# A planner's computed order replaced by a written table, with 24 GpSimd maxima tied to VectorE's place

## The chip, the cores and the metric

The kernel runs on one core of one Trainium2 chip. The time is that of one execution on the device, in microseconds (us); three executions of the kernel before gave 1046.39, 1047.41 and 1048.51, median 1047.41.

## The reference, cut to what is computed

```python
# attention: batch 8, heads 8, seq 576, head_dim 64, 128 features
def phi(x):
    proj = einsum('bhsd,df->bhsf', x, w_phi)
    proj = proj - max(abs(proj), axis=-1)
    return concatenate([exp(proj), exp(-proj)], axis=-1)
q_p, k_p = phi(q), phi(k)
kv  = einsum('bhsf,bhsd->bhfd', k_p, v);  z = sum(k_p, axis=2)
attn = einsum('bhsf,bhfd->bhsd', q_p, kv) / (einsum('bhsf,bhf->bhs', q_p, z) + 1e-6)
# feed-forward on 4608 tokens, 512 -> 2048 -> 512, weights as 64-bit words
x = attn as (batch*seq, heads*head_dim)
return gelu(x @ w_in) @ w_out
```

## The kernel before

The program is a list of 3,662 operations, created in a fixed order and numbered from 0: 914 of TensorE (one may be up to 80 matmuls), 933 of ScalarE, 1,209 of VectorE, 68 of GpSimd and 538 of SyncE, which issues nearly all DMAs. `Plan.op` notes for each its engine, cost, buffers and rank. `Plan.order` then simulates all engines with the costs written at the top of the class, and picks at each step the operation of lowest rank that can go; the ranks contain a hand-written table DELAY of offsets. `Plan.emit` sorts by the planned start and writes the instructions; every engine keeps that order. Semaphore waits between engines follow from the data and buffers alone. So what a run does is set by five orders, one for each engine, and by how long each operation waits for another engine.

The work has these parts, named as in the traces:

- **Attention, k side** (`k_unit`, `k_quad`): TensorE projects a part of k (pk, in PSUM); VectorE takes the maximum over features (mx, L465) and subtracts it (ek, L401), both reading PSUM; ScalarE takes two exponentials (L470); TensorE sums k with v (kv), ScalarE copies it to kvn.
- **Attention, q side** (`q_front`, `q_pair`, `q_rest`): TensorE projects q transposed (pq), ScalarE copies it to SBUF (pc, L395), GpSimd takes the maximum over partitions (mb, L539, `partition_all_reduce`), VectorE subtracts (pc<-pc,mb, two operands in SBUF), ScalarE takes two exponentials (ef, L544), TensorE forms numerators (pn) and, for the first three batches, denominators (dn), which ScalarE copies to xo and do. Later batches sum denominators on GpSimd (db, L550). A maximum has one of three sizes: 288 columns (batch 0), 512 ("main") and 64 times four ("rest").
- **Weights** (`split_weight`): each of 32 pieces w_i*, w_o* is loaded (raw), unpacked from 64-bit words by ScalarE (L416) and four VectorE steps (wt, L417, L419, L421, L423), and split in a high and a low part (ScalarE cast, VectorE subtraction at L401). The last piece of w_in is w_i3_3.
- **Feed-forward** (`tokens`, `up`, `block`, and from the ninth block `seven`): for each of 18 blocks of 256 tokens, 12 matmuls for each of 16 column groups (ph), gelu twice on ScalarE, their difference on VectorE (gl, L401, reading PSUM), and po. Batch after batch of attention feeds it.
- **Weight sums** (`sums_of_weights`): ts, on VectorE and ScalarE, used by the later blocks.

Of the kernel before, what the change touches and what calls it, by code (L numbers as in the profile page):

```python
# [62 lines left out]
class Plan:  # L63


    HOP = {"pe": 0.2, "act": 0.14, "dve": 0.13, "pool": 0.1, "sp": 0.05}
    SAME = {"pe": 0.0, "act": 0.0, "dve": 0.127, "pool": 0.1, "sp": 0.0}
    SWITCH = 1.3

    BEHIND = {"f": 0.1, "k": 0.1, "q": 0.095, "v": 0.09, "w": 0.09, "n": 0.1, "d": 0.05, "z": 0.09}  # L70
    BEFORE = {"f": 0.08, "k": 0.1, "q": 0.1, "v": 0.05, "w": 0.05, "n": 0.05, "d": 0.1, "z": 0.04}
    SHAPE = {"f": 0, "k": 1, "q": 1, "v": 2, "n": 2, "w": 3, "d": 4, "z": 5}
    READS = {"max": 1.15, "add": 2.45, "max main": 2.1, "add main": 4.43, "max rest": 1.05, "add rest": 2.15}
    WRITES = {"max": (1.4, 2.02), "add": (2.75, 3.47), "max main": (2.3, 3.42), "add main": (4.6, 5.97), "max rest": (1.2, 1.83), "add rest": (2.4, 3.1)}
    SPENT = {"max": 2.14, "add": 3.59, "max main": 3.54, "add main": 6.11, "max rest": 1.94, "add rest": 3.23}
    WINDOW = 3.413
    BUSY = 0.8
# [5 lines left out]

    def turn(self, a, b):
        return self.BEHIND[a] + self.BEFORE[b] + (0.09 if a == "f" and b != "d" else 0.0)

# [47 lines left out]
    def order(self, bias):  # L134
        free = dict(self.slots)
        slot_free_at = {t: [0.0] * n for t, n in self.slots.items()}
        turn = dict.fromkeys(self.slots, 0)
        engines = {}
        for o in self.ops:
            engines.setdefault(o.eng, [])  # L140
        clock = dict.fromkeys(engines, 0.0)
        table = [None]
        cand = {e: [] for e in engines}
        for o in self.ops:
            if o.wait == 0:
                cand[o.eng].append(o)
        done = []
        n = len(self.ops)

        gelus, left_at, dma, dge = [0], [0.0], [0.0], [0.9]  # L150
        port = [0.0]

        def start_of(o):
            t = max(clock[o.eng], o.ready)
            if o.table == "exp" and table[0] == "gelu" and gelus[0] % (2 * STICK):
                t = max(t, left_at[0] + PATIENCE)
            seen = {}
            for b in o.bufs:
                if not b.held and b.tag is not None:
                    f, i = slot_free_at[b.tag], seen.get(b.tag, 0)  # L160
                    if len(b.line) <= i or b.line[i] is not b:
                        return None
                    when = f[(turn[b.tag] + i) % len(f)]
                    if when is None:
                        return None
                    t = max(t, when)
                    seen[b.tag] = i + 1
            if o.eng == "dve":
                for a, z, least in port[1:]:
                    if o.port >= least and a <= t < z:  # L170
                        t = z
            return t


        clk = {"i": 0, "full": False, "busy": 0.0}
        last, first = ["f"], {}

        def run(t, work, duty):
            while work > 1e-9:
                i = int(t / self.WINDOW + 1e-9)  # L180
                while clk["i"] < i:
                    use = clk["busy"] / self.WINDOW
                    clk["full"] = use > (0.5 if clk["full"] else self.BUSY)
                    clk["i"] += 1
                    clk["busy"] = 0.0
                speed = 1.0 if clk["full"] else 0.51
                dt = min((i + 1) * self.WINDOW - t, work / speed)
                clk["busy"] += dt * duty
                work -= dt * speed
                t += dt  # L190
            return t

        while len(done) < n:
            best = None
            for e, lst in cand.items():
                if not lst:
                    continue
                opts = []
                for o in lst:
                    t = start_of(o)  # L200
                    if t is not None:
                        opts.append((t, o))
                if not opts:
                    continue
                t0 = min(t for t, _ in opts)
                lim = max(t0, clock[e]) + 0.02
                hold = 0.0
                if e == "pe" and last[0] == "f":
                    t_of = {id(o): max(o.ready, first.setdefault(o.n, t)) for t, o in opts}
                    there = [o for t, o in opts if t <= lim and o.kind != "f"]  # L210
                    if sum(o.cost for o in there) < LUMP and all(lim - t_of[id(o)] < LINGER for o in there):
                        hold = 4000.0
                key = None
                for t, o in opts:
                    if t <= lim:
                        k = o.rank
                        if e == "act" and o.table is not None and o.table != table[0]:
                            k += bias
                        if o.kind != "f":
                            k += hold  # L220
                        if key is None or (k, o.n) < key[0]:
                            key = ((k, o.n), t, o)
                if best is None or key[1] < best[1] or key[1] == best[1] and e == "pool":
                    best = key
            if best is None:
                raise RuntimeError("no operation can go")
            _, t, o = best
            cand[o.eng].remove(o)
            cost = o.cost
            if o.eng == "act" and o.table is not None and o.table != table[0]:  # L230
                cost += self.SWITCH
                table[0] = o.table
            if o.eng == "pe":
                if self.SHAPE[last[0]] != self.SHAPE[o.kind]:
                    cost += self.turn(last[0], o.kind)
                last[0] = o.kind
            o.start = t
            if o.eng == "pool" and o.port:
                t = max(t, port[0])
                a, z = self.WRITES[o.port]  # L240
                port[1:] = [(t, t + self.READS[o.port], 1), (t + a, t + z, 2)]
            o.end = run(t, cost, o.duty) if o.eng == "pe" else t + cost
            if o.nbytes:
                dge[0] = max(dge[0], t) + 0.55
                dma[0] = max(dma[0], dge[0] + 0.75) + o.nbytes / RATE
                o.late = dma[0] + 0.15 + DMASLACK - o.end
            if o.table == "gelu":
                gelus[0] += 1
                left_at[0] = o.end
            clock[o.eng] = o.end  # L250
            if o.eng == "dve" and o.port:
                port[0] = o.end
            for b in o.bufs:
                if b.tag is not None and not b.held:
                    f = slot_free_at[b.tag]
                    b.slot = turn[b.tag]
                    f[b.slot] = None
                    turn[b.tag] = (b.slot + 1) % len(f)
                    b.held = True
                    assert b.line.pop(0) is b  # L260
                b.left -= 1
                if b.left == 0 and b.tag is not None:
                    slot_free_at[b.tag][b.slot] = o.end + o.late + self.HOP[o.eng] + (PESLACK if b.tag in self.banks else 0.0)
            for u in o.users:
                u.wait -= 1
                u.ready = max(u.ready, o.end + o.late + (self.HOP if u.eng != o.eng else self.SAME)[o.eng] + (POOLSLACK if o.eng == "pool" else 0.0) + (PESLACK if u.eng == "pe" and o.eng != "pe" else 0.0))
                if u.wait == 0:
                    cand[u.eng].append(u)
            done.append(o)
        self.done = done  # L270
        return max(o.end + o.late for o in done)

    def emit(self):
        todo = sorted(self.done, key=lambda o: (o.start, o.n))
        parts = [o.part for o in todo if o.eng == "pe"][1:] + [None]
        for o in todo:
            if o.eng == "pe":
                self.then = parts.pop(0)
            if o.reopen and self.turn_over is not None:
                self.turn_over()  # L280
                self.turn_over = None
# [731 lines left out]
SUMSAT = 175.933  # L1013
# [72 lines left out]
```

## Time and profile before

| what | value |
|---|---|
| median of three executions | 1047.41 us |
| the profiled execution | 1048.43 us |
| its span, first to last instruction | 1046.6 us |
| TensorE busy | 1019.6 us |
| VectorE busy | 661.1 us |
| ScalarE busy | 614.5 us |
| GpSimd busy | 276.9 us |
| mean granted TensorE clock | 0.993 |

Times in the trace count from the start of the span; 1.83 us of the profiled execution lie outside it. Lines such as L401 belong to helpers used for many operations, so an operation is known by its tile (ph, mx, wt_o) and its time.

### The profile page before, as it was taken

The numbers are of one execution on the slowest core, as the hardware profiler recorded it, in microseconds if no ns is written. First come the engines' busy times: TensorE is split into PE (matmuls) and PEld (weight loads), VectorE is DVE, ScalarE is ACT, GpSimd is POOL, SyncE is SP. The second block draws the span as 40 slices with busy tenths as digits, with TensorE's granted clock in tenths as the row PEclk, the third lists the DMA queues.
The fourth block names the chain that finished last, engine by engine and source line by source line (L and its number), as shares of the span: only waits on it lengthen the run. The fifth ranks groups of instructions, "written<-read, shape, count | busy, mean of one in ns | idle before, by whom it ended". The sixth has DMA issues, their size and how long they took to land.

```text
span 1046.6 us, 24197 instructions
## 1 busy us (share of the span) xinstructions
PE 1019.6 (97%) x10070; PEld 893.1 (85%) x10070; DVE 661.1 (63%) x1209; ACT 614.5 (59%) x1011; POOL 276.9 (26%) x72
## 2 busy tenths in 40 slices
PE   6889998999999999999999999999999999999998
PEld 5555776878878878897887889999999999999998
DVE  5899999987777854334643433555564556474754
ACT  5788888886768766757755642343243334243433
POOL 2343331373376352326566540000000000000000
PEclk9899999999999999999999999999999999999999
DMA  8775654524534433222321339201111111110000
GB/s 294 216 231 170 208 189 119 164 88 140 162 123 147 152 108 91 67 76 72 97 72 39 97 107 326 60 22 41 44 39 40 43 42 42 41 42 19 24 22 21
DMA packets 87327, 107.11 MB, mean 102 GB/s; under 512 B 29021, under 2 KB 57245, under 8 KB 87217
## 3 DMA queue, kind: packets, MB, share of 16 engines
q1 hardware_dynamic: 86928, 105.30, 32.7%
q8 instruction: 79, 1.29, 0.5%
q14 instruction: 32, 0.25, 0.1%
q10 hardware_dynamic: 288, 0.26, 0.1%
HBM read 75.87 MB, written 29.66 MB: 101 GB/s over the span
## 4 chain that ended last, share of the span: by engine, by line
PE 90%; DVE 5%; ACT 2%; issue 1%; DMA 1%; SPq 0%; DVEq 0%; ACTq 0%
PE ph L360 38%; PE po L360 17%; PE pa L360 10%; PE pb L360 7%; PE kv L360 6%; PE pn L360 4%; PE pk L360 3%; PE pq L360 3%; PE dn L360 1%; DVE wt_i L421 1%; PE pn_rest L360 1%; DMA vt<-in_va_dram 1%; DVE ek L401 0%; DVE wt_i L423 0%; DVE pc L401 0%
## 5 line engine op out<-in xcount | busy, mean ns | idle before, releaser
L360 PE MATMUL ph<-xh,w_i 128*128 128x256 f32 x2304 | 416.6, 278 | 0.0
L360 PEld LDWEIGHTS ph<-xh,w_i 128*128 128x128 f32 x2304 | 357.1, 188 | 9.0 <-issue 5.1
L360 PE MATMUL ph<-xl,w_i 128*128 128x256 f32 x1152 | 319.3, 277 | 0.0
L360 PEld LDWEIGHTS ph<-xl,w_i 128*128 128x128 f32 x1152 | 217.2, 189 | 0.3
L539 POOL PARTITION_ALL_REDUCE mb<-pc x36 | 120.6, 3356 | 202.3 <-ACT pc L395 153.3
L360 PE MATMUL po<-w_o,gh 128*128 128x512 f32 (+1 forms) x519 | 162.4, 395 | 0.0
L550 POOL PARTITION_ALL_REDUCE db<-pc x20 | 124.2, 6212 | 93.7 <-DVE pc L600 89.9
L360 PEld LDWEIGHTS po<-w_o,gh 128*128 128x128 f32 x519 | 93.3, 188 | 30.0 <-issue 8.5
L401 DVE TENSOR_TENSOR sg<-ga 128x256 f32<-128x256 f32 (+1 forms) x240 | 84.3, 376 | 54.1 <-ACT ga L839 50.3
L360 PE MATMUL pa<-w_o,oh 128*128 128x256 f32 x640 | 112.6, 276 | 0.0
L401 DVE TENSOR_TENSOR gl<-ph,gh 128x512 fp32r<-128x512 f32 x64 | 43.5, 687 | 90.7 <-ACT ph L750 90.6
L360 PE MATMUL po<-w_o,gl 128*128 128x512 f32 (+1 forms) x275 | 100.8, 378 | 0.0
L360 PEld LDWEIGHTS pa<-w_o,oh 128*128 128x128 f32 x640 | 96.3, 188 | 0.1
L839 ACT ACTIVATE ga<-ph 128x512 f32<-128x512 f32 x80 | 47.8, 597 | 82.3 <-PE ph L360 52.1
L401 DVE TENSOR_TENSOR ul<-sg,uh 128x384 fp32r<-128x384 f32 x80 | 44.6, 558 | 71.5 <-ACT uh L395 70.3
L360 PE MATMUL pa<-w_o,ol 128*128 128x256 f32 x320 | 88.3, 276 | 0.0
L360 PE MATMUL pb<-tw,uh 128*128 128x256 f32 x464 | 82.9, 276 | 0.1
L544 ACT ACTIVATE ef<-pc 128x1024 f32<-128x1024 f32 (+1 forms) x72 | 68.1, 973 | 14.2 <-DVE pc L401 10.3
L470 ACT ACTIVATE ek<-ek 128x1024 f32<-128x1024 f32 x64 | 67.6, 1059 | 11.1 <-DVE ek L401 10.2
L395 ACT CAST uh<-sg 128x384 fp32r<-128x384 f32 x80 | 41.0, 512 | 50.6 <-PE pb L360 25.3
L360 PEld LDWEIGHTS pb<-tw,uh 128*128 128x128 f32 x464 | 69.9, 188 | 0.3 <-DVE ob L401 0.3
L360 PE MATMUL pn<-ef,kvn 128*64 128x512 f32 (+1 forms) x288 | 64.9, 571 | 1.9 <-ACT do L395 0.8
(93 smaller groups left out, 1591.5 us busy)
## 6 DMA issues: line engine op xcount, KB each, us to landing
vt<-in_va_dram SPq DMA_DIRECT2D x32, 325.0 KB
t_d<-ts SPq DMA_DIRECT2D x40, 256.0 KB
out_dram<-ob SPq DMA_DIRECT2D x34, 256.0 KB
kt<-in_kT_dram SPq DMA_DIRECT2D x32, 256.0 KB
raw_i<-in_w_in_dram SPq DMA_DIRECT2D x16, 512.0 KB
raw_o<-in_w_out_dram SPq DMA_DIRECT2D x16, 512.0 KB
qt<-in_qT_dram SPq DMA_DIRECT2D x28, 256.0 KB
x_d<-xo SPq DMA_DIRECT2D x28, 256.0 KB
```

The lines of the kernel that those rows point to most:

```text
L360: return tc.keep_in_program_order(nc.tensor.matmul(*a, **kw))
L395: op(eng, cost, lambda: nc.scalar.copy(out=dst(), in_=src()), r=r, w=w, **kw)
L401: op(eng, cost, lambda: e.tensor_tensor(out=dst(), in0=a(), in1=b(), op=o), r=r, w=w, **kw)
L421: op("dve", dve(512), lambda: v.scalar_tensor_tensor(out=t(), in0=low(), scalar=29, in1=t(), op0=ALU.logical_shift_right, op1=ALU.bitwise_ ...
L470: op("act", act(256 * n), lambda s=s: nc.scalar.activation(e[s](), e[1](), AF.Exp, scale=1.0 - 2.0 * s), r=[e[1]], w=[e[s]], table="exp", ...
L539: op("pool", plan.SPENT[most], lambda: nc.gpsimd.partition_all_reduce(mb(), pc(), P, bass_isa.ReduceOp.absmax), r=[pc], w=[mb], port=most, ...
L544: op("act", act(2 * n), lambda s=s: nc.scalar.activation(ef[s](), pc(), AF.Exp, scale=1.0 - 2.0 * s), r=[pc], w=[ef[s]], table="exp", **k())
L550: op("pool", plan.SPENT[total], lambda: nc.gpsimd.partition_all_reduce(db(), pc()[:, :2], P, bass_isa.ReduceOp.add), r=[pc], w=[db], port= ...
L839: op("act", act(2 * TB, True) + 0.037, lambda ph=ph, ga=ga: nc.scalar.activation(ga(), ph(), AF.Gelu), r=[ph_all], w=[ga], table="gelu", a ...
```

## The change

`Plan.order` no longer simulates. It reads ORDER, a table of all 3,662 operation numbers, and `Plan.emit` writes them in this order. The ranks, DELAY and the planner's costs are left in part but nothing reads them. The operations themselves, their buffers (HOME is untouched) and their shapes are the same. Place by place, 177 of TensorE's 914 places hold another operation than before, 357 of ScalarE's 933, 442 of VectorE's 1,209, 320 of SyncE's 538, and 2 of GpSimd's 68. The last place that differs on VectorE is the 505th, which runs 422 us after the start in the trace before.

A second table, TOGETHER, has 24 pairs, a GpSimd maximum and a VectorE operation that reads PSUM (mx, ek, er or gl). The maximum gets one more semaphore wait: for the VectorE operation just ahead of the named one.

```diff
-    def order(self, bias):
...
+    def order(self):
+        self.done = [self.ops[int(n)] for n in ORDER.split()]
+        assert len({o.n for o in self.done}) == len(self.ops)
 
     def emit(self):
-        todo = sorted(self.done, key=lambda o: (o.start, o.n))
+        todo = self.done
+        together = dict((int(n) for n in pair.split(":")) for pair in TOGETHER.split())
+        beside, ahead, last = set(together.values()), {}, None
...
+            if o.n in beside:
+                ahead[o.n] = last
             ins = o.fn()
             if not isinstance(ins, list):
                 self.tc.keep_in_program_order(ins)
+            if o.eng == "dve":
+                last = ins
+            if o.n in together:
+                self.tc.add_manual_dep(ins.ins, ahead[together[o.n]].ins.name, mybir.DependencyInfo(mybir.DependencyClass.Sync, mybir.DependencyReason.DATA),
+                                       reason="reads while VectorE reads PSUM")
...
-    total = plan.order(bias=BIAS)
...
+    plan.order()
     plan.emit()
...
-DELAY = {
...
+DELAY = {}
...
+ORDER = """
+0 3 2 9 1 4 45 58 30 13 27 157 5 11 6 10 46 71 7 47 14 15 28 59 60 16 17 8 31 189 158 20 165 18 32 48 29 49 50 51 12 19 52 159 21 181 419 33 166 197
...
+TOGETHER = """
+61:6 74:39 87:416 117:424 130:468 143:469 440:475 453:531 484:540 497:1328 514:548 556:584 569:1342 613:1363 630:1356 674:664 690:1403 726:1410
+742:1417 762:1452 808:843 876:924 896:1754 942:1768
+"""
```

In the first line of ORDER, 3 is the load of the first k piece (kr), 2 that of the projection's weights (wst), 9 the first kt, 45 and 58 two qt; 4 is TensorE's first operation, pk_r.

## Rows read from the trace of the kernel before

**Rows 1.** The page: the span, and part 1, each engine's busy time.

```profile
span 1046.6 us, 24197 instructions
...
PE 1019.6 (97%) x10070; PEld 893.1 (85%) x10070; DVE 661.1 (63%) x1209; ACT 614.5 (59%) x1011; POOL 276.9 (26%) x72
```

**Rows 2.** Busy time by stretch: us from:to, length, each engine's, granted clock, DMA.

```profile
0.00:25.00 25.00, 16.51 (x284) 14.13 (x286) 14.44 (x18) 13.88 (x19) 5.02 (x7) 0.93 0.88 307
25.00:50.00 25.00, 20.32 (x358) 14.21 (x354) 20.72 (x31) 19.19 (x37) 7.13 (x4) 0.86 0.68 206
50.00:75.00 25.00, 20.79 (x398) 14.39 (x392) 23.79 (x30) 20.32 (x35) 13.90 (x5) 1.00 0.71 228
75.00:100.00 25.00, 22.76 (x245) 14.46 (x241) 23.64 (x34) 21.99 (x33) 9.62 (x3) 0.93 0.56 164
100.00:150.00 50.00, 50.00 (x591) 36.82 (x588) 48.00 (x78) 43.20 (x65) 15.15 (x4) 1.00 0.66 205
150.00:200.00 50.00, 46.97 (x592) 36.22 (x592) 48.02 (x77) 44.43 (x68) 10.15 (x4) 1.00 0.41 124
```

**Rows 3.** TensorE's timeline, five operations that waited: start, us, operation, [idle before <-releaser].

```profile
6.31 1.23 PE L360 MATMUL pk_r<-wst,kr 64*128 64x128 f32 x8 [6.31 <-DMA wst<-in_w_st_dram]
...
40.52 2.29 PE L360 MATMUL pq<-qt,wst 64*128 64x288 f32 x8 [2.95 <-DVE ek L401]
...
61.19 0.69 PE L360 MATMUL kv<-vt,er 128*64 128x65 f32 x16 [2.33 <-DMA vt<-in_va_dram]
...
83.69 1.29 PE L360 MATMUL dn<-ef,kvn 128*32 128x256 f32 x16 [2.24 <-ACT do L395]
...
159.22 1.07 PE L360 MATMUL dn<-ef,kvn 128*32 128x256 f32 x16 [1.73 <-ACT xo L395]
```

**Rows 4.** TensorE's busy time and granted clock in two short stretches.

```profile
40.02:46.85 6.83, 6.33 (x40) 0.50 0.73 214
84.40:87.81 3.41, 3.41 (x22) 0.50 0.68 180
```

**Rows 5.** SyncE's timeline: the first DMA issues, that of wst, one of vt.

```profile
0.72 0.86 SPq L563 DMA_DIRECT2D qt<-in_qT_dram  x2
...
3.09 0.43 SPq L390 DMA_DIRECT2D wst<-in_w_st_dram  x1
...
55.61 0.85 SPq L496 DMA_DIRECT2D vt<-in_va_dram  x1
```

**Rows 6.** ScalarE's timeline, three operations.

```profile
82.74 0.62 ACT L395 CAST w_i<-wt_i 128x512 fp32r<-128x512 f32 x1 [0.94 <-DVE wt_i L423]
83.27 0.37 ACT L395 COPY do<-dn 128x256 f32<-128x256 f32 x1
...
158.58 0.58 ACT L395 COPY xo<-pn 128x512 f32<-128x512 f32 x1
```

**Rows 7.** VectorE's timeline, six operations.

```profile
24.70 1.52 DVE L419 TENSOR_SCALAR wt_i<-wt_i 128x512 uint32<-128x512 uint32 x1
...
139.26 0.69 DVE L421 SCALAR_TENSOR_TENSOR wt_o<-raw_o,wt_o 128x512 uint32<-128x512 uint32 x1
...
146.07 2.56 DVE L421 SCALAR_TENSOR_TENSOR wt_o<-raw_o,wt_o 128x512 uint32<-128x512 uint32 x1
...
149.15 0.68 DVE L423 SCALAR_TENSOR_TENSOR wt_o<-raw_o,wt_o 128x512 uint32<-128x512 uint32 x1
...
154.57 2.26 DVE L421 SCALAR_TENSOR_TENSOR wt_i<-raw_i,wt_i 128x512 uint32<-128x512 uint32 x2
...
186.97 1.21 DVE L465 TENSOR_REDUCE mx<-pk 128x8 f32<-128x1024 f32 x1
```

**Rows 8.** GpSimd's timeline, two of the 43 maxima.

```profile
145.90 3.54 POOL L539 PARTITION_ALL_REDUCE mb<-pc  x1 [2.55 <-ACT pc L395]
...
186.61 3.54 POOL L539 PARTITION_ALL_REDUCE mb<-pc  x1 [3.79 <-DVE pc L401]
```

**Rows 9.** VectorE's busy time up to the end of w_i3_3's split.

```profile
0.00:168.77 168.77, 148.78 (x214) 0.96 0.67 215
```

More of the change, by code (lines that the diff above doesn't have):

```diff
@@ L63 @@
 class Plan:
[L66 to L74, printed above, removed]
     SPENT = {"max": 2.14, "add": 3.59, "max main": 3.54, "add main": 6.11, "max rest": 1.94, "add rest": 3.23}
-    WINDOW = 3.413
-    BUSY = 0.8
     def __init__(self, tc):
@@ L82, in __init__ @@
         self.tc, self.ops, self.slots, self.lines, self.stream, self.since, self.unit = tc, [], {}, {}, None, 0.0, "start"
-    def turn(self, a, b):
-        return self.BEHIND[a] + self.BEFORE[b] + (0.09 if a == "f" and b != "d" else 0.0)
     def pool(self, pool, tag, bufs):
@@ L132, in op @@
         return o
-    def order(self, bias):
[L135 to L271, printed above, removed]
@@ L929, in fused_kernel @@
             seven(j, tw, lambda x, t=t, d=d: t + d * x, earlier if j == SEVEN else ())
-    total = plan.order(bias=BIAS)
-    if VERBOSE:
-        print("planned", total, {e: sum(o.cost for o in plan.done if o.eng == e) for e in ("pe", "dve", "act", "pool", "sp")})
+    plan.order()
     plan.emit()
-DELAY = {
[40 rows of a table removed]
-}
+DELAY = {}
 HOME = {
@@ L1012 @@
 SUMS = 2
-SUMSAT = 175.933
-SUMSEACH = 3.384
+SUMSAT = 190.75
+SUMSEACH = 4.989
 SUMSPAN = 581.86
@@ L1017 @@
 T18 = 997.68
-BIAS = 551.516
-STICK = 2
-PATIENCE = 2.138
 URGE = -1000.0
 EARLY = 41.32
-WPACE = 4.989
+WPACE = 4.81
 WSPAN = 48.9
@@ L1028 @@
 ND = 3
-LUMP = 82.289
-LINGER = 6.494
 PAIR_K = 0.224
@@ L1034 @@
 LEAD = 85.26
-HOLD = 23.07
+HOLD = 32.35
 WR = -23.78
@@ L1038 @@
 AT = 175.45
-PESLACK = 0.03
-POOLSLACK = 0.3
-DMASLACK = 0.517
 T0 = 85.1
-RATE = 285.0
-VERBOSE = False
+ORDER = """
[115 rows of a table added]
+"""
+TOGETHER = """
+61:6 74:39 87:416 117:424 130:468 143:469 440:475 453:531 484:540 497:1328 514:548 556:584 569:1342 613:1363 630:1356 674:664 690:1403 726:1410
+742:1417 762:1452 808:843 876:924 896:1754 942:1768
+"""
 _ARGS = ["qT", "kT", "va", "w_st", "w_in", "w_out"]
```

154 rows, old and new, of tables (DELAY, ORDER) are left out of this document.

## The prediction

> **What bounds the kernel now.** I read the page's totals first: TensorE is busy 1019.6 of 1046.6 us [rows 1], so about 27 us is all that any order can win from its idle time, and VectorE, busy 63% overall, looks harmless. The totals mislead about the start, so the stretches came next [rows 2]. TensorE idles 8.49, 4.68, 4.21 and 2.24 us in the four quarters of the first 100 us, nothing from 100 to 150, 3.03 from 150 to 200; that is 22.65 us, nearly all of it. In the same stretches VectorE is the fuller engine: 23.79 and 23.64 of 25 us, then 48.0 of 50 twice. Before 170 us there are thus two chains of nearly equal length, and an order must shorten both. TensorE's own timeline then names its waits [rows 3]: 6.31 us for the load of wst, 2.95 for an ek that frees a PSUM buffer, 2.33 for a load of vt, 2.24 and 1.73 for copies by ScalarE. These five are 15.56; the other 7.09 of the 22.65 lies in shorter pieces. Last, the granted clock: at 40.02 and again at 84.40, each just after one of these waits, it stands at 0.50, the 1.2 GHz level, for 6.83 and 3.41 us [rows 4].
>
> **The start.** Five issues precede that of wst, the first at 0.72 and wst at 3.09 [rows 5], 0.474 us each. In the table wst is SyncE's second. Its landing moves by four issues, 1.9 us, if it still takes as long to land. The new first load, kr, is needed by the same matmul, so nothing else replaces it. Bounds: 0, if the landing is what the first DMA of a program costs, and 1.9. I take 1.9.
>
> **The waits that the table dissolves.** I compared TensorE's order with those of the engines that it waits for. At 40.52 the pq waits for the ek of batch 1's first pk. The new order issues that pk one place sooner and puts a pn between it and the pq; 2.95 goes if VectorE is not later there, of which below. At 83.69 dn waits for the copy "do", which stands behind a w_i cast that itself waited 0.94 us for VectorE [rows 6]; the new order has the copy ahead of that cast. At 159.22 it is the same with "xo", after the cast of w_i1_3; it too moves ahead. At 61.19 kv waits for a vt whose buffer comes free only when the preceding kv ends, so its issue at 55.61 [rows 5] can hardly be sooner; but it takes 5.5 us to land, with a raw weight issued just ahead of it. That raw moves from SyncE's 58th place to its 29th, so the vt should land sooner; I take 1.8 of the 2.33 and keep 0 as the lower bound. Together 2.95 + 2.24 + 1.73 + 1.8 = 8.7. Of the shorter pieces, 7.09 in all, I take those whose operations change places, about a quarter, 1.6; bounds 0 and 7.1.
>
> **The clock.** 6.83 + 3.41 = 10.24 us ran at half speed with TensorE nearly always busy [rows 4], so at 2.4 GHz the same work takes 5.1 us less. Both stretches follow a wait of this list. I take 4.0, the longer one whole and half of the shorter; bounds 0 and 5.1.
>
> TensorE's side sums to 1.9 + 8.7 + 1.6 + 4.0 = 16.2 us. The matmuls are the same; changes between kinds of matmul fall from 200 to 193, costed at nothing since back-to-back matmuls leave TensorE full in rows 2.
>
> **VectorE's ceiling.** The seventh pair of column groups of block 0 needs all of w_i3_3, whose split ends VectorE's 214th operation at 168.77 [rows 9]. Four things move that moment. The start: 1.9. The work ahead: the new table has it at place 210; an mx and three small steps of a quotient go behind it, 1.2 [rows 7] plus about 0.4, 1.6. The idle time: 168.77 - 148.78 = 20.0 us [rows 9], of which some 7 precede the first projection's results (it starts at 6.31 [rows 3]). Of the other 13 the longest piece waits for ScalarE to unpack w_o1, and that step moves five places up; I take 5 in all, bounds 0 and 13. And the stretched operations. A wt step that takes 0.69 alone takes 2.56 when a main maximum is running beside it [rows 7, 8]; from the first at 24.70 to the last at 154.57, twelve operations before 168.77 are stretched by 13.0 us together. Beside another maximum an mx, which reads PSUM, takes its plain 1.21 [rows 7, 8]. That is what TOGETHER is after. How long does a maximum block? The stretched step started 0.17 after the maximum's start and ended 2.73 after it; less its own 0.69, it resumed at 2.04, though the maximum lasted 3.54. A step that started 3.25 after it took 0.68 [rows 7, 8]. So only the first 2 us of a main maximum must be covered. Of a small one it is half as much: the two steps at 154.57, beside a maximum of a rest, take 2.26 where two plain ones take about 1.3 [rows 7]. The table covers them with mx and ek (2.3 us), one of them (1.1) or one gl (0.6); adding what stays uncovered for the pairs before w_i3_3, and 1.5 for maxima without a pair, leaves about 7 of the 13.0. I take 6 won, bounds 0 and 13. VectorE's side is 1.9 + 1.6 + 5 + 6 = 14.5 us: less than TensorE's 16.2, so it rules.
>
> The Trainium skill, page "SBUF — State Buffer", section "Who interferes with whom", says that the port pair shared by VectorE and GpSimd is an exclusive lock, held for the whole instruction. Where the trace shows 2.04 of 3.54 us it differs from that, and the measurement decides; that a VectorE operation with one input in SBUF is not held agrees with the mx above. By the page's rule a cover of 0.6 to 2.3 us would leave the rest of each maximum to block.
>
> **The added waits.** Behind a waiting maximum GpSimd has only later maxima; who waits for it is pc<-pc,mb, then ef, then pn. Set against the trace of before, 14 of the 24 awaited operations had ended over 1.5 us before the maximum began, and cost nothing; three fall within 0.25 us; seven end later than the maximum began. One of these is the maximum at 145.90: its awaited step ends at 149.83, 3.9 us later [rows 7, 8]. TensorE's long wait after it, at 159.22, is for another chain [rows 3], so its pn came in time, and the table moves consumers back where the wait is longest. I cost them at nothing on the path, bounds 0 and 7 x 3.9 = 27 if all reach TensorE. A table of this size must also make new short waits somewhere: I allow 0.5, no less than the smallest gaps that stay.
>
> **Sum.** 14.5 - 0.5 = 14.0 us. Against the profiled execution's own 1048.43 (1046.6 span and 1.83 around it) that gives 1034.4. This execution lay 1.0 above the median of the runs shown; between 1033.4 and 1034.4 I take 1034.0. After 170 us TensorE was full in every stretch but a short end, so what is won stays won.
>
> **The rivals.**
>
> *VectorE gains little.* If the waits do not place the maxima beside PSUM reads (the 14 are already satisfied, and a maximum then starts where its pc copy ends), the stretches stay at 13.0. VectorE's side falls to 1.9 + 1.6 + 5 = 8.5 and 1048.4 - 8.5 + 0.5 gives 1040.4. For it: rows 8 show a maximum beside an mx by chance already. Against it: the order too can place them.
>
> *The gain is given back.* TensorE arrives early and waits for weights or loads between 150 and 200; it wins the start alone or nothing, 1046 to 1048. For it: VectorE is 96% busy there. Against it: w_i3_3's four fewer operations ahead.
>
> *A maximum locks VectorE out to its end.* Were each two-input step held to the end of 3.54 us, the covers would leave about 22 us before w_i3_3 in place of 13.0. VectorE's side would be 8.5 - 9 = -0.5: 1048.9, no change. The step at 149.15 speaks against it [rows 7]. This is the rule of the Trainium skill's page named above.
>
> *Slower: the added waits starve TensorE.* If maxima that wait 3.9 us each pass it on to pn, and four of the seven do, 15.6 us is lost and the whole gain is gone; at five, 19.5, less 14, gives 1053. It decides in favour of slower from the fourth on. Against it: in rows 3 no long wait is for an ef.
>
> **How the numbers follow.** Chances: forecast (1029 to 1039) 0.52; VectorE gains little (1039 to 1044) 0.25; better than forecast, because stretches or clock return more, below 1029, 0.06; given back 0.05; locked out 0.03; slower 0.09. Three executions of before spread over 2.1 us, so 0.2% is about what a measurement can tell. Faster by more than that is 0.52 + 0.25 + 0.06 and a fifth of "given back", 0.84; within it 0.07; slower 0.09. The range leaves out the last three and a little more: 1028 to 1043.
>
> **What would show it.** pk_r starts near 4.4 us in place of 6.31. TensorE's idle time in the first 100 us falls from 19.6 to about 9, and the waits for ek, do and xo named above are gone. The clock is not at 0.50 near 40 us. w_i3_3's split ends near 154 in place of 168.77. VectorE's steps stretched beyond twice their length before that are about half as long in sum. Wrong would make it: a GpSimd row that waits for VectorE followed by a pn that waits for ef; or TensorE idle between 100 and 200 us where it was full.

## The result, and the profile after

The changed kernel is slower by half a percent: 1052.92 us (median of 4 runs, 1051.54 to 1054.73) against 1047.18 for the kernel before in the same session; ratio 1.0055, 95% interval 1.0033 to 1.0076. The forecast was 1034.0, in a range from 1028 to 1043. The profiled execution took 1054.06 us.

The page of the changed kernel: span, busy time, and the group of part 5 that waited most.

```profile
span 1052.3 us, 24204 instructions
...
PE 1020.1 (97%) x10088; PEld 894.1 (85%) x10088; DVE 682.8 (65%) x1209; ACT 609.1 (58%) x1011; POOL 274.7 (26%) x72
...
L220 PE MATMUL ph<-xh,w_i 128*128 128x256 f32 x2304 | 420.3, 279 | 9.7 <-DVE gl L261 9.7
```

The last line has no counterpart before: 9.7 us in which the up-projection (ph) waits for the product gl, which frees a PSUM bank of ph. The stretches tell where:

```profile
0.00:25.00 25.00, 18.07 (x352) 14.90 (x354) 17.93 (x22) 16.61 (x23) 6.83 (x7) 1.00 0.83 300
25.00:50.00 25.00, 21.99 (x414) 15.56 (x414) 23.56 (x37) 22.29 (x44) 7.40 (x4) 1.00 0.78 259
50.00:75.00 25.00, 21.22 (x324) 12.17 (x324) 24.32 (x34) 21.08 (x36) 11.61 (x5) 1.00 0.72 207
75.00:100.00 25.00, 25.00 (x277) 18.51 (x271) 23.22 (x37) 22.91 (x34) 8.24 (x3) 1.00 0.71 204
...
100.00:180.00 80.00, 76.84 (x968) 58.13 (x965) 75.42 (x115) 69.29 (x107) 22.46 (x7) 1.00 0.54 168
180.00:350.00 170.00, 159.15 (x1566) 128.69 (x1565) 138.33 (x190) 109.02 (x162) 80.48 (x18) 0.97 0.39 120
```

Against [rows 2], TensorE's first 100 us idle 13.72 us in place of 19.62, and the granted clock stays at 1.00. From 180 to 350 us it idles 10.85, where it had been full, as this window of the kernel before shows:

```profile
180.00:350.00 170.00, 170.00 (x1727) 138.28 (x1726) 138.99 (x208) 128.55 (x186) 86.45 (x19) 1.00 0.44 137
```

These lines of TensorE's timeline are the longer waits, first at the start, then in the later part (us from the start, us, operation, the idle time ahead and what ended it):

```profile
3.27 1.22 PE L220 MATMUL pk_r<-wst,kr 64*128 64x128 f32 x8 [3.27 <-DMA wst<-in_w_st_dram]
...
62.46 0.70 PE L220 MATMUL dn<-ef,kvn 128*32 128x144 f32 x16 [1.42 <-ACT xo L255]
...
71.78 1.13 PE L220 MATMUL pq<-qt,wst 64*128 64x512 f32 x4 [1.68 <-DMA qt<-in_qT_dram]
...
193.83 0.39 PE L220 MATMUL ph<-xh,w_i 128*128 128x256 f32 x1 [3.34 <-DVE gl L261]
...
236.28 0.58 PE L220 MATMUL ph<-xh,w_i 128*128 128x256 f32 x1 [3.17 <-DVE gl L261]
...
329.76 0.38 PE L220 MATMUL ph<-xh,w_i 128*128 128x256 f32 x1 [2.42 <-DVE gl L261]
```

Of the five waits of [rows 3] the first is 3.27 now, and the others are gone or below 0.6. Three new ones of 3.34, 3.17 and 2.42 us stand where nothing stood. After the first two the granted clock is at 0.50 (windows of the changed kernel):

```profile
195.31:202.14 6.83, 6.14 (x42) 3.21 (x42) 6.66 (x12) 2.68 (x4) 0.69 (x1) 0.50 0.37 124
236.27:239.68 3.41, 3.40 (x14) 3.30 (x15) 3.41 (x8) 1.03 (x3) 0.32 (x1) 0.50 0.82 254
```

Why is gl late? VectorE's timeline at the three places, with one plain ts product (185.00) for comparison:

```profile
185.00 0.42 DVE L261 TENSOR_TENSOR ts<-ts 128x256 fp32r<-128x256 f32 x1
...
188.55 4.63 DVE L261 TENSOR_TENSOR ts<-ts 128x256 fp32r<-128x256 f32 x1 [0.28 <-ACT ts L255]
193.10 0.68 DVE L261 TENSOR_TENSOR gl<-ph,gh 128x512 fp32r<-128x512 f32 x1
...
230.70 4.93 DVE L261 TENSOR_TENSOR ts<-ts 128x256 fp32r<-128x256 f32 x2
235.55 0.68 DVE L261 TENSOR_TENSOR gl<-ph,gh 128x512 fp32r<-128x512 f32 x1
...
324.41 4.69 DVE L261 TENSOR_TENSOR ts<-ts 128x256 fp32r<-128x256 f32 x2 [0.32 <-ACT ts L255]
329.02 1.28 DVE L261 TENSOR_TENSOR gl<-ph,gh 128x512 fp32r<-128x512 f32 x2
```

And GpSimd's beside it:

```profile
188.36 6.11 POOL L410 PARTITION_ALL_REDUCE db<-pc  x1 [6.78 <-DVE pc L460]
...
230.11 6.48 POOL L410 PARTITION_ALL_REDUCE db<-pc  x1 [7.49 <-DVE pc L460]
...
323.58 6.48 POOL L410 PARTITION_ALL_REDUCE db<-pc  x1 [5.08 <-DVE pc L460]
```

Each time a ts product with both inputs in SBUF starts 0.2 to 0.8 us behind one of GpSimd's sums (db, not a maximum), takes 4.3 to 4.6 us in place of 0.42, and gl stands directly behind it in VectorE's order. GpSimd's sum is released by VectorE's pc step ("<-DVE pc L460"). In the order of before, the gl of b1_1 and b1_5 stand ahead of or directly behind that pc step, the gl of b2_7 one ts of another form behind it; the new table puts one to three ts products between the step and gl. Nothing about maxima or the added waits occurs in this chain.

### The profile page after: what moved, and what is told of

The parts are those of the page before. It is cut to its first block, busy times and chain, and to the rows that moved or that the text cites. A ratio compares the mean times of both kernels' runs of the same rounds, so it can differ in the third digit from the quotient of the medians.

```text
span 1052.3 us, 24204 instructions
## 1 busy us (share of the span) xinstructions
PE 1020.1 (97%) x10088; PEld 894.1 (85%) x10088; DVE 682.8 (65%) x1209; ACT 609.1 (58%) x1011; POOL 274.7 (26%) x72
## 4 chain that ended last, share of the span: by engine, by line
PE 69%; DVE 1%; ACT 1%; issue 1%; DMA 0%; DVEq 0%; ACTq 0%
PE ph L220 31%; PE po L220 12%; PE pa L220 10%; PE pb L220 7%; PE kv L220 3%; PE pn L220 2%; PE pq L220 1%; PE pk L220 1%; DVE ts L261 0%; PE pn_rest L220 0%; DVE ob L261 0%; PE pq_rest L220 0%; DMA t_d<-ts 0%; PE pc L220 0%; ACT ek L330 0%
## 5 line engine op out<-in xcount | busy, mean ns | idle before, releaser
L399 POOL PARTITION_ALL_REDUCE mb<-pc x36 | 118.1, 3284 | 206.8 <-ACT pc L255 133.0
L220 PE MATMUL kv<-vt,ek 128*64 128x65 f32 x2048 | 65.7, 222 | 0.7 <-ACT ek L330 0.5
```

What stands on the lines that cost most here:

```text
L220: return tc.keep_in_program_order(nc.tensor.matmul(*a, **kw))
L399: op("pool", plan.SPENT[most], lambda: nc.gpsimd.partition_all_reduce(mb(), pc(), P, bass_isa.ReduceOp.absmax), r=[pc], w=[mb], port=most, ...
```

## The experiments

The theory that forms from this (A): the first part of the change is sound, and the loss comes from three ts products that a sum holds ahead of a gl, with the low clock after them. The rival (B): TensorE's lead can't be held in any order, because it then waits for VectorE, weights or loads elsewhere. Numbers below are operation numbers of ORDER; 1403 is gl of b1_0, 1410 gl of b1_1, 1438 gl of b1_5, 1726 and 1727 the second gelu and gl of b2_7; 1472, 1497, 1592 and 1595 are ts products. The kernel before was 1046.11, 1047.10 and 1047.33 us by its medians in the three sessions below; ratios are to it.

**Halves of the table.** In words, since the tables are long:

```diff
 # e1_new_then_old
-ORDER: the new table
+ORDER: the new table up to 1403 (178 us), then the rest in the order of before
 # e2_old_then_new
+ORDER: the order of before up to the same place, then the rest in the new order
```

> The new table up to the gl of the first pair of block 1 (176 to 178 us in the trace after), the order of before from there on, with the added waits of the first part alone. Theory A (the first part of the table wins about 9 us and its later part loses about 14, because VectorE steps held by GpSimd's sums stand ahead of the gl that TensorE waits for): 1038, between 1035 and 1042, and no TensorE wait for gl over 2 us between 180 and 340. Theory B (whatever is won before 180 us is given back, because weights, loads and VectorE cannot be earlier): 1045 to 1048. Theory W (the added waits are the loss): no nearer than A, since the first part keeps 17 of them; slower than 1047.

> The reverse: the order of before up to the same gl, the new table from there on, with the added waits of that part. Theory A: the start wins nothing and the later part still loses its 10 to 14 us, so 1057 to 1062. Theory B: the later part is not at fault, 1046 to 1049. Theory W: only 7 waits are left, about 1049.

e1 took 1052.32 (ratio 1.0048, 1.0029 to 1.0067), a miss for A, but the test was unclean: 18 operations that the new table defers past 1403, twelve of them DMAs, come due at the joint. Between 179 and 201 us TensorE waited 2.58 us for a gl, 4.36 for a load of vt that is one of the 18, and 2.39 for an exponential whose chain waited for another of them. At the products gl up to the joint it had led by 4.0 to 8.7 us (5.0 at the last); after it it was 5.8 late to the end. So e1 decides nothing between A and B. e2 took 1061.68 (1.0139, 1.0107 to 1.017), as A had it: level before the joint, 17 us late after it, with waits before ph of 3.29, 3.11 and 2.41 us. So the later part of the table loses 14 to 17 us behind either first part. (e1 kept 16 of the pairs and e2 8, one away from the counts in their expectations.)

**The waits.**

```diff
 # e3_new_without_waits
-TOGETHER = (24 pairs)
+TOGETHER = (none)
 # e4_old_with_waits: the order of before, and
+TOGETHER = (the 19 pairs that this order allows)
```

> The whole new table without the 24 added waits. Theory A: the waits decide little, 1050 to 1056; VectorE steps stretched by maxima before 158 us grow by a few us. Theory W: the loss goes, 1047 or less. If the waits were what wins the first part, it gets slower, 1056 or more, and w_i3_3's split ends past 160.

> The order of before with 19 of the 24 added waits (for the other five the awaited step stands behind the maximum in this order and they are left out). Theory A: nearly nothing, 1045 to 1049, since only a few of these waits end after the maximum could start. Theory W: slower by several us, 1050 or more.

e3: 1055.79 (1.0079, 1.0054 to 1.0104), the same three waits of TensorE (3.10, 2.94, 2.25). e4: 1046.85 (0.9998, 0.9978 to 1.0019). The waits are not the cause of the loss. What they are worth in the new order is not shown: e3 led by 5.0 us at the gl of b1_0, where the changed kernel led by 8.6, but e1, with nearly all of the waits of this part, led by 5.0 too, and the intervals of e3 and of the changed kernel overlap. In the old order they are worth nothing.

**Three gl ahead of the held products, and one alone.**

```diff
 # e8_one_gl_first: the first pair only; e5_three_gl_first: all three
-1414 1472 1410 685
+1414 1410 1472 685
-1499 1497 745 ... 1438
+1499 1438 1497 745
-1592 1595 1726 ... 1727
+1726 1727 1592 1595
```

> The new table, with three VectorE products that free a PSUM bank of ph (gl of b1_1, b1_5 and b2_7; for the last the gelu too) put ahead of the ts product that stood directly before them and that GpSimd's sum held for 4.6 us. Theory A (these three held ts products cost TensorE its three waits before ph, 3.34, 3.17 and 2.42 us, and the low clock after them, 10.2 us at half, so 5.1): the three waits go, the clock stays full, and the time falls by 9 to 14 us, to 1039 to 1044. Rival B (the lead cannot be held whatever the order, TensorE waits elsewhere for the same work, for weights or loads): the three waits go but others come within the next 100 us, time 1050 or more. Rival C (the sum only moves its hold to the gl's own successor and the wait comes one gl later): waits before ph of over 2 us at b1_2, b1_6, b3_0.

> The new table with only the first of the three products moved (gl of b1_1 ahead of the ts product of s2). Theory A: the wait of 3.34 us before ph at 190 us and the 6.8 us of half clock after it (3.4 us lost) go, the two later waits stay: 1046 to 1049, 4 to 7 us below the new table. Rival B: no gain over the new table, 1051 to 1054.

e5: 1046.29 (0.9994, 0.9979 to 1.001), 6.6 us below the changed kernel. e8: 1052.79 (1.0052, 1.0029 to 1.0076), no gain, and a miss for A. VectorE's timeline of e5 shows why the first move is worth nothing, and the line of TensorE below it what waited instead:

```profile
187.64 0.69 DVE L261 TENSOR_TENSOR gl<-ph,gh 128x512 fp32r<-128x512 f32 x1
188.25 4.33 DVE L261 TENSOR_TENSOR ts<-ts 128x256 fp32r<-128x256 f32 x1
192.50 1.21 DVE L325 TENSOR_REDUCE mx<-pk 128x8 f32<-128x1024 f32 x1
193.74 1.23 DVE L261 TENSOR_TENSOR ek<-pk,mx 128x1024 f32<-128x1024 f32 x1
```

```profile
195.07 1.00 PE L220 MATMUL pk_r<-wst,kr 64*128 64x128 f32 x8 [3.81 <-issue]
```

gl goes first, and the ts product still takes 4.33 us; now the maximum mx and the subtraction ek behind it are late. ek ends at 194.97, and pk_r starts 0.10 later, after 3.81 us of idle time where it had been 0.69 ("issue": the view names no releaser; that it is ek, the last reader of pk, is inferred and tested next). This is rival C of the expectation in kind: the wait moves to the next reader of PSUM, though it comes before pk_r (3.82 us in e8) and not before a later ph. The other two moves bring nearly all of the 6.6.

**The held product behind the reader of pk too.**

```diff
 # e9_ts_behind_key_maximum, against e5 (717 is ek<-pk,mx)
-1410 1472 685 713 716 717 1420
+1410 685 713 716 717 1472 1420
```

> The kernel of e5 (the new table, three gl ahead of the held ts) with the first of these ts products (s2, 0.42 us plain, 4.33 held beside a sum) moved on by two more VectorE operations, behind the maximum over pk and the subtraction that frees pk's PSUM bank. Theory A (the sums hold a VectorE operation with two SBUF operands, and what is lost is set by what stands directly behind it): the wait of 3.81 us before pk_r at 191 us and the half clock of 3.41 us after it go; the lead of 9 to 11 us is kept, 1037 to 1041 by the median. Rival B (TensorE gives its lead back elsewhere whatever is moved): 1045 to 1048, another wait of over 2 us between 190 and 330 us.

1041.25 (0.9944, 0.9921 to 0.9967), faster than before. VectorE there:

```profile
188.90 0.69 DVE L261 TENSOR_TENSOR gl<-ph,gh 128x512 fp32r<-128x512 f32 x1
189.63 1.23 DVE L325 TENSOR_REDUCE mx<-pk 128x8 f32<-128x1024 f32 x1
190.89 1.23 DVE L261 TENSOR_TENSOR ek<-pk,mx 128x1024 f32<-128x1024 f32 x1
192.03 1.80 DVE L261 TENSOR_TENSOR ts<-ts 128x256 fp32r<-128x256 f32 x1
193.76 1.66 DVE L457 TENSOR_SCALAR pc<-ef,kvn 128x512 f32<-128x512 f32 x1
```

mx and ek, which read PSUM, run at their plain length beside the sum (it starts at 189.02), and the ts waits out the rest of the hold with nobody behind it. The stretch from 180 to 350 us of e9:

```profile
180.00:350.00 170.00, 167.76 (x1748) 137.59 (x1748) 149.46 (x206) 118.59 (x177) 86.89 (x20) 1.00 0.44 133
```

TensorE idles 2.24 us there in place of 10.85, at full clock: three places of the order (three gl, a gelu and a ts moved) are 11.7 us, from 1052.92 to 1041.25.

**The sums left out.** The order stays as it is; three of GpSimd's twenty sums are replaced by a constant, so the denominators of three pieces are not computed.

```diff
 # e10_three_sums_as_memsets
+        if nm in ("3_0_0", "3_2_0", "4_2_0"):
+            op("pool", ..., lambda: nc.gpsimd.memset(db(), 4.0), ...)
+        else:
```

> The new table with its order untouched; three of GpSimd's twenty sums (those at 188, 230 and 324 us) are left out, and GpSimd fills db with a constant there instead, so that the denominators of these three pieces are not computed. Theory A (GpSimd's sum is what holds the ts product, not the ts product's own wait or data): the three ts products take below 1 us, the three waits before ph and the low clock after them go, 1037 to 1044. Rival D (the order itself starves TensorE there: the gl comes too late in VectorE's queue with or without a hold): the waits stay above 2 us each, 1050 to 1054.

1039.50 (0.9923, 0.9899 to 0.9947). The same ts and gl of b1_1, in the same order:

```profile
188.71 0.43 DVE L261 TENSOR_TENSOR ts<-ts 128x256 fp32r<-128x256 f32 x1 [0.28 <-ACT ts L255]
189.05 0.68 DVE L261 TENSOR_TENSOR gl<-ph,gh 128x512 fp32r<-128x512 f32 x1
```

The ts product is back to 0.43, and TensorE's three waits before ph are gone (0.37 is the longest left). Rival D falls: the order alone starves nobody; order and sum together do.

**The first part alone.**

```diff
 # e6_cut_at_78us, e7_cut_at_117us
-ORDER: the new table
+ORDER: the new table up to 78 (117) us, then the order of before; 9 (13) of the 24 pairs
```

> The new table up to about 78 us (337 operations), then the order of before; at this joint only 5 operations are in another place, so nothing is owed. Nine of the waits are left. Theory A (the first part of the change is sound, the loss is three places of its later part): the lead of about 9 us at 90 us is kept to the end, 1036 to 1040. Rival B (what is won at the start is given back anyway, as TensorE runs ahead of its weights or of VectorE): the lead shrinks to below 2 us by 250 us, 1044 to 1047.

> The new table up to about 117 us (545 operations), then the order of before, 5 operations owed at the joint, thirteen of the waits left. Theory A: the lead of 8 to 10 us is kept to the end, 1036 to 1040. Rival B: given back by 250 us, 1044 to 1047.

e6: 1040.26 (0.993, 0.9913 to 0.9947). Its lead is 8.86 us at the gl of b0_6 (175 us) and 8.85 at that of b5_1 (460): what is won at the start is kept if the later order is that of before. Rival B falls as a rule. e7: 1045.17 (0.9998, 0.998 to 1.0016), a miss for A, for another reason, which VectorE's and TensorE's timelines of e7 show:

```profile
127.57 0.18 DVE L525 TENSOR_SCALAR dc<-dc 128x32 f32<-128x32 f32 x1 [2.61 <-DMA dc<-d_d]
```

```profile
130.34 1.13 PE L220 MATMUL pq<-qt,wst 64*128 64x512 f32 x4 [3.20 <-DVE ek L261]
```

A small step of a quotient waits 2.61 us for its load at the head of VectorE's queue, with the ek that frees pk's bank behind it. In e6 the same step, 3.7 us earlier, did not wait.

**The reverse.** The kernel of e6 with three ts products put directly ahead of a gl beside a sum.

```diff
 # e11_cut_with_three_holds, against e6
-1438 797 1499
+1499 1438 797
-1727 928 ... 1595
+1595 1727 928
-1699 820 ... 1559
+1559 1699 820
```

> The reverse: the kernel of e6 (the new table to 78 us, then the order of before, 1040.26) with three ts products of its later part (s8, s20 and s27) put directly ahead of a gl that stood before them, each beside one of GpSimd's sums (at 221, 278 and 310 us in the run of e6). Nothing else is changed. Theory A: the ts products take 3 to 5 us, the gl behind them come 2.5 to 4.5 us later, TensorE waits before ph in two or three places, 4 to 9 us in all, and 2 to 5 us go with the half clock after them: 1045 to 1053. Rival B (TensorE has slack there that takes it up): 1039 to 1042.

1040.45 (0.9929, 0.9905 to 0.9953): no loss, a miss for A as I had put it. Two of the three products slipped through at 0.69 and 0.68 us (they started before the sum did). The third was held, but TensorE did not notice. VectorE, then TensorE:

```profile
311.41 4.64 DVE L261 TENSOR_TENSOR ts<-ts 128x256 f32<-128x256 f32 x1
315.97 1.27 DVE L261 TENSOR_TENSOR gl<-ph,gh 128x512 fp32r<-128x512 f32 x2
```

```profile
315.35 1.16 PE L220 MATMUL pk<-wst,kt 64*128 64x128 f32 x16
316.44 0.72 PE L220 MATMUL po<-w_o,gh 128*128 128x512 f32 x2
...
319.31 0.28 PE L220 MATMUL ph<-xh,w_i 128*128 128x256 f32 x1
```

gl frees its bank at about 316.6; between pk and the next ph TensorE has 2.9 us of po to do (316.44 to 319.31). In the changed kernel the same ph comes directly behind pk and waits 2.42 us at 329.76. So by this case a hold costs only where TensorE's order, too, asks for the bank at once. The kernel before, which was full from 180 to 350 us, has the same case; GpSimd's sum, then the held ts and the gl directly behind it:

```profile
208.59 6.15 POOL L550 PARTITION_ALL_REDUCE db<-pc  x1 [2.75 <-DVE pc L600]
```

```profile
209.31 4.14 DVE L401 TENSOR_TENSOR ts<-ts 128x256 fp32r<-128x256 f32 x1
213.37 0.68 DVE L401 TENSOR_TENSOR gl<-ph,gh 128x512 fp32r<-128x512 f32 x1
```

That second condition was missing from theory A; a run that puts it alone into the order of before was not made.

## Why the prediction was wrong

**The step that failed** is the sentence "After 170 us TensorE was full in every stretch but a short end, so what is won stays won." It read the order of before's later part and applied it to a table that changes this part too, up to 422 us. The lead over the kernel before, 8.6 us at the gl of b1_0 (178 us), had become 5.6 us of delay by that of b5_1 (467 us): 14.2 us lost. Of these 10.85 are idle time of TensorE; the other 3.4 I put down to the low clock, whose price e10, with the same order and no half clock there, lets one read (TensorE in the changed kernel, then in e10):

```profile
196.27 1.22 PE L220 MATMUL pk_r<-wst,kr 64*128 64x128 f32 x8 [0.69 <-issue]
...
203.90 0.73 PE L220 MATMUL po<-w_o,gh 128*128 128x512 f32 x2
```

```profile
192.22 0.71 PE L220 MATMUL pk_r<-wst,kr 64*128 64x128 f32 x8
...
197.23 0.73 PE L220 MATMUL po<-w_o,gh 128*128 128x512 f32 x2
```

From pk_r to po it took 7.63 us in place of 5.01, 2.62 more; from 236.28 to 240.73 us twelve matmuls of ph and seven of po took 4.45 where e10 needs 2.74 (226.28 to 229.02), 1.71 more; together 4.3, somewhat above the 3.4. I had counted the operations that a maximum stretches, and not one that a sum stretches, though a sum lasts 6.11 us. Summed over all VectorE operations of the first 420 us that ran beside a reduction, what they took above the plain length of their kind grew from about 32 us to over 50, those beside sums from 14 to 28. But e9 has nearly as much, 24 to 27 beside sums, and is 11.7 us faster: it is the place of a held operation that costs, not the amount. The planner that the diff deletes had the hold of a sum among its costs ("add main": 4.43 in READS); the trace has 188.55 + 4.63 - 188.36 - 0.42 = 4.40.

**The start** (1.9): right in kind, 3.04 measured (6.31 to 3.27). The issue of wst moved as forecast, from 3.09 [rows 5] to 1.23; the other 1.2 us came from its landing, 2.04 us after its issue in place of 3.22, which the prediction had held fixed.

**The waits that the table dissolves** (8.7 + 1.6): the four named ones went, 9.25 (what stands at their places is counted with the shorter pieces). But the shorter pieces, of which I had taken a quarter as won, grew: idle time up to 180 us is 13.72 + 3.16 = 16.9, less the 3.27 of the start 13.6, where it had been 7.1 by [rows 2, 3]. So TensorE's idle time up to 180 us fell by 5.8, not by 12.2. A wait that is dissolved leaves the next one behind it; two of 1.42 and 1.68 us are shown above.

**The clock** (4.0): right in kind, no half clock before 180 us. The prediction missed a third stretch of the kernel before, which [rows 2] show as 0.93 in the first quarter:

```profile
12.72:16.13 3.41, 3.41 (x38) 3.19 (x36) 1.88 (x3) 1.63 (x2) 2.48 (x2) 0.50 1.04 398
```

The size fits as well as like operations tell: pq, pn, dn and pk from 40.52 us took 7.2 us, the same forms in the changed kernel 4.6, and the stretch at 84.40 cost about 1.5, together some 4. TensorE's total busy time fell by only 2.4, from 1019.6 [rows 1] to 1017.2 in e9 and e6, but that is no price of the clock: e6 has 3.41 us of half clock of its own from 151.62, and what else changed in the total is open.

**VectorE's ceiling** (14.5, w_i3_3 near 154): its split ends at 157.61, 11.2 us sooner than in [rows 9]. This window of the changed kernel ends there:

```profile
0.00:157.61 157.61, 140.73 (x2067) 99.97 (x2068) 144.88 (x211) 132.50 (x210) 50.88 (x22) 1.00 0.70 222
```

Busy time fell by 3.9 us and idle time by 7.3, where I had 5 for the idle time. The stretches beside maxima fell from 13.0 to about 10.4, not to 7: the waits cover less than I took. Yet the ceiling was none: TensorE never waited for w_i3_3, and the lead of 8.6 at the gl of b1_0 is its own: 5.8 of idle time and 2.8 of busy time, where the clock gave back some 4 and something else, which no run separates, took part of it. Nor was VectorE the fuller engine in all the stretches named: from 100 to 150 us it was TensorE, 50.00 against 48.00 [rows 2].

**The added waits** (nothing on the path): right as far as e3 and e4 tell.

The sum of the first part was thus 14.0 where the lead came to 8.6, which is 5.4 short, and 14.2 was lost later: 5.4 + 14.2 = 19.6 of the 19.7 us between 1054.06 and the 1034.4 that the sum gave. The rival "The gain is given back" had the effect, and named 150 to 200 us; the waits ran from 190 to 330, were for VectorE and not for weights or loads, and took more than the gain. "The added waits starve TensorE" had the sign and the wrong mechanism. "A maximum locks VectorE out to its end" fell again: on the Trainium skill's page "SBUF — State Buffer", section "Who interferes with whom", the lock lasts the whole instruction; beside a sum the trace shows 4.40 of 6.11 us, and the measurement decides.

What stays open is how much more of the 14.0 can be had. e10 (1039.50), e6 (1040.26) and e9 (1041.25) end 6 to 8 us below before; each has 16.5 to 18 us of idle time left in TensorE's first 350 us, 3.3 of it at the start and the rest in pieces of at most about 1.7, and no run here tried to move those.

## What to carry to other kernels

When an order changes, read its later part as closely as the part that it is meant to mend; "full before" says nothing of a stretch whose order changes too. List every long operation that holds another engine (here the sums as well as the maxima), and ask of each what the new order puts directly behind the operation that it holds: a reader of PSUM that TensorE needs next must go ahead of it. Splicing the old and the new order finds the guilty part quickly where few operations are owed at the joint: e1 owed 18 and decided nothing, e6 owed 5 and is faster than either kernel. Even so e7, which owed 5 as well, lost some 5 us of lead, most of it to the late load at 127 us.

## What was not expected of the hardware

The hold of a sum is not one piece. In e9 a TENSOR_SCALAR that starts 4.74 us after the sum's start (193.76 against 189.02) takes 1.66 us where its like at 196.47 takes 0.48, although the ts ahead of it had just come free; so in its last part the sum holds another kind of operation. By this row the hold ends 193.76 + 1.66 - 0.48 - 189.02 = 5.92 us after the sum's start, nearly at the sum's end. The planner that the diff deletes knew of this part too ("add main": 4.6 to 5.97 in WRITES).
